# S5 state-space layer beside a Mish MLP: dense-1 weights of all seven groups prepared in one earlier block

## The chip, the cores and the metric

The kernel runs on one core of one Trainium2 chip. The metric is the device time of one launch in microseconds (us). A core has a matrix engine (PE, with its weight loads shown as PEld), a vector engine (VE; the profile calls it DVE), a scalar engine (ACT), a general engine (POOL) and a queue engine (SP) that only issues transfers. Each runs its own list of instructions in order and waits on semaphores; ACT, POOL and SP also issue DMAs from their places in that list, so a DMA waits for whatever stands ahead of it there.

## The reference

With x of 2048 rows and 1024 columns, and xn its layer norm over the columns, three terms are added:

```python
xn = _layernorm(x)
# state space: 1024 complex states, diagonal recurrence over the 2048 rows
Lam_bar = exp(dt * Lam)
B_bar = ((Lam_bar - 1.0) / Lam)[:, None] * Bmat
Bu = einsum("bld,pd->blp", xn, B_bar)
h[t] = Lam_bar * h[t - 1] + Bu[t]
y = 2.0 * einsum("blp,dp->bld", h, Cmat).real + xn * Dskip
# dense, 1024 -> 3584 -> 1024
a = einsum("bsd,df->bsf", xn, w1) + b1
act = a * tanh(softplus(a))                  # Mish
out = x + y + einsum("bsf,fd->bsd", act, w2)
```

Types are bf16 in and out.

## The kernel before, in words

**Blocks.** The rows are worked in four blocks of 512. The text counts them 1 to 4; in the code `blk` is 0 to 3. Each block has these stages on PE: dense 1 (x times w1, 28 tiles f of 128 columns), the input product (x times B, real and imaginary), dense 2 (Mish output times w2) and the output product (states times C, `proj`, three of whose eight slices j come last and finish the rows quarter by quarter). Between the input and the output product VE rotates the input (`rotate_in`), runs the recurrence as a scan (`recur`, eight slices j) and rotates back. Dense 2 and the output product add into the same eight banks of PSUM; `finish` adds them to x in `xx`, and the rows are stored.

**Quarter products.** A product of a 1024-deep operand can be made from four half-size pieces by Winograd's form of Strassen's scheme: seven products of half the width instead of eight. The input product is done so from block 2 on (`product`, `evacuate`, L871 to L939), dense 1 for some groups of four tiles (`w_product`, `w_evacuate`, L945 to L1019). The seven products of a group are numbered 1 to 7; letters in the order strings name the group: a to d are pairs of slices of the input product, p q s w x y z the seven groups of w1. The left operands are sums of parts of xnT, four arrays TT made by `sums_x`. The right ones (units) are prepared once: the group's 1024x512 of w1 is loaded in four quarters (`w_load`, POOL), its magnitude found (`w_abs`, ACT), carried across partitions through DRAM (`w_row_out`, `w_row_in`), turned into a power of two (`w_exponent`, VE), used to scale the quarters in place (`w_scale`, ACT), and three of the four scaled quarters are stored to DRAM (`wsd`, units 1, 2, 4); VE makes four sums in f16 (`w_sums`, units 5, 6, 3, 7), also stored. Later blocks read the units through the ring.

**Who prepares what, before.** Block 2 does dense 1 plainly (28 tiles) and prepares groups 3 to 6. Block 3 does groups 0 to 2 plainly (12 tiles, `NPL`), groups 3 to 6 by quarter products, and prepares groups 0 to 2 after its dense 2 has freed `act`. Block 4 does all seven by quarter products. Some sums of groups 0 and 1 are kept as closures and run as VE steps `k` in block 4; stores that aren't urgent are kept in `held` and `later`.

**The ring.** Weights come through `ring`, seven slots of 2048 columns. `items` lists all loads in order of use (w1, units `ws`, w2, and `c`, the rescaled C); `item_done` issues the load seven items ahead, on SP, into the slot just freed. SP also issues the transposes: x after its layer norm (`transpose_dma`), B (`transpose_B`), C (`transpose_C`). All of these share one order.

**Block 1.** Its first seven tiles are computed on raw x for the first 256 rows and corrected (`raw_scale`, `raw_add`, `hraw`). The tables of sines and cosines come from POOL phases (`phases`) and ACT (`table`). After phase 3, POOL issues the loads of x of block 2, whose statistics VE makes at tiles 14, 16, 18, 20 (`ln_stats_only`). During dense 2, VE runs the recurrence and scales C (`scale_C`), then B is scaled to a common range per state (`rows_scale`, `rows_spread`, `scale_B`), with two small DMAs on POOL for each half, and ACT writes the rescaled C to DRAM (`rows_C`).

**Layer norm of the next block.** In blocks 2 and 3 ACT makes the statistics (`next_stats`), the root (`next_root`, with two VE operations) and the scaled rows (`next_scale`); SP transposes them. `ln_skip` (VE) adds the skip term.

**The order inside a block** is written by hand in strings such as

```python
    WHOLE = HEAD + " d3 c7 d7 u7 c4 r2 u5 d4 u6 u4 r3 r4 r5 r6 r7"
```

where r is a rotation, u an early piece of dense 2, g a Mish over a range of tiles. `side(f)` hangs other work between the tiles of dense 1.

Of the kernel before, what the change touches and what calls it, by code (L numbers as in the profile page):

```python
# [5 lines left out]
ALU = mybir.AluOpType  # L6
# [3 lines left out]
P = 128  # L10
# [153 lines left out]
def build_kernel(nc, A_x, A_Lambda_re, A_Lambda_im, A_B_re, A_B_im, A_C_re, A_C_im,  # L164
# [21 lines left out]
    WHOLE = HEAD + " d3 c7 d7 u7 c4 r2 u5 d4 u6 u4 r3 r4 r5 r6 r7"  # L186
# [3 lines left out]
    PARTS = "a2 a1 b2 b1 a5 b5 a6 b6" + LATE  # L190
    FULL = ("p1 p5 k0 p2 k0 q1 q5 p6 q2 k0 s1 p7 k0 s5 p3 k0 q6 k0 s2 k0 p4 q7 k0 q3 h0 s6 q4 g0 a2 a1 s7 s3 b2 b1 s4 g1 a5 b5 a6 b6" + LATE)
    QUADS = "pqswxyz"
    NWQ = len(QUADS)
    NV = NPL // 4
    assert NV == 3
    W_BANKS = ((0, 2, 1), (3, 2, 4), (7, 2, 6), (3, 5, 7), (1, 5, 6), (4, 5, 7), (3, 5, 6))
    PLACE = {blk: (3, 4, 5, 6, 2, 0, 1) if blk == NB - 1 else (0, 1, 2, 3, 4, 5, 6) for blk in range(NB)}

    def w_items(order, place):
        units = [(place[QUADS.index(o[0])], int(o[1])) for o in order.split() if o[0] in QUADS]  # L200
        return [("ws", tuple(units[i:i + 2])) for i in range(0, len(units), 2)]

    W_ITEMS = {blk: w_items(FULL if blk == NB - 1 else PARTS, PLACE[blk]) for blk in SPLIT}

# [100 lines left out]
    wsm_v = late("wsm_v", [P, 4, NV], f32, 0)  # L305
    wsm_w = late("wsm_w", [P, 4, NWQ - NV], f32, 192)

    def wsm(n, lo, hi):
        return wsm_v[:, n, lo:hi] if lo < NV else wsm_w[:, n, lo - NV:hi - NV]

# [6 lines left out]
    ROWS = ((NV, NV + 2), (NV + 2, NWQ), (0, NV))  # L317
    wmd = [nc.dram_tensor("wmd%d" % h, [P, hi - lo], f32, kind="Internal").ap() for h, (lo, hi) in enumerate(ROWS)]
    b_wmd = [Buf("wmd%d" % i) for i in range(len(ROWS))]
    b_wmx = [Buf("wmx%d" % i) for i in range(len(ROWS))]  # L320
# [70 lines left out]
    for blk in range(NB):  # L391
        n1 = 0 if blk == NB - 1 else NPL if blk in SPLIT else NF
        items += [("w1", g) for g in range(n1 // 2)]
        items += W_ITEMS.get(blk, [])
        items += [("w2", 2 * PLACE[blk][g // 2] + g % 2) for g in range(NF // 2)]
        items += [("c", j) for j in range(NJ)] if blk >= FAST else []
# [280 lines left out]
    for b in [b for bs in b_wsm + b_ln + b_si_i + [b_sbf, [b_rv]] for b in bs]:  # L677
        b.readers = dict(b_st.readers)
# [55 lines left out]
    def turns():  # L734
# [3 lines left out]
        small("xc", "xs", "xc", ALU.max)  # L738
        aop(lambda e: e.activation(c("s1"), c("xs"), AF.Sin, scale=TWO_PI, bias=kon[:, 1:2]),
# [78 lines left out]
    def first_tile(blk, f):  # L818
        bank = f % 8
        if blk in SPLIT:  # L820
            bank = (0, 1, 2, 3, 5, 1, 4, 0, 6, 2, 3, 7)[f]
# [13 lines left out]
        if raw and f == 0:  # L835
            aop(lambda e: e.activation(act[:, 0:NR, 0:2 * P], hraw[:, 0:NR, :], AF.Mish),
                reads=b_hbf[0:4], writes=b_actf[0:NR])
# [3 lines left out]
    def places(blk, f, n):  # L841
        if blk in SPLIT:
            return (hb[:, f:f + n, :], b_hbf[f:f + n]) if f < NPL else (act[:, f - NPL:f - NPL + n, :],
                                                                        b_actf[f - NPL:f - NPL + n])
        return act[:, f:f + n, :], b_actf[f:f + n]
# [99 lines left out]
    def w_product(blk, i, n):  # L945
# [4 lines left out]
        s, half = n_item[0] % NRING, units.index((PLACE[blk][i], n))  # L950
# [20 lines left out]
    def w_evacuate(blk, i, n, keep):  # L971
        X, Y, Z = W_BANKS[i]
        at = PLACE[blk][i]
# [52 lines left out]
    W_RAW = (("a", 0), ("a", 8), ("h", 8), ("h", 0), ("h", 8), ("a", 0), ("a", 8))  # L1026
    W_SUM = (("a", 22), None, ("a", 16), ("a", 16), ("a", 22), ("a", 16), ("a", 22))
    held, later, steps = [], [], []

    def w_sum_at(i):  # L1030
        if i == 1:
            return [("a", 20), ("h", 12), ("h", 14), w_raw(i, 1, 0)]
        kind, t = W_SUM[i]
        return [(kind, t + 2 * n) for n in range(3)] + [w_raw(i, 1, 0)]
# [20 lines left out]
    def w_abs(i):  # L1055
        if i < NV:
            kind, t = w_raw(i, 0, 0)
            v, b_v = (hb, b_hbf) if kind == "h" else (act, b_actf)
            aop(lambda e: e.activation(CT[:, :, 1, TB:D], v[:, t:t + 8, :], AF.Abs, accum_out=wsm(0, i, i + 1)),  # L1059
                reads=b_v[t:t + 8], writes=b_snap + [b_wsm[0][i]])  # L1060
            return
        for ci in range(2):
            src, b_src = w_half(i, ci)
            aop(lambda e, src=src, ci=ci: e.activation(
                CT[:, 0:4, 1, TB:D], src.rearrange("p (j t) -> p j t", j=4), AF.Abs, accum_out=wsm(ci, i, i + 1)),
                reads=b_src, writes=b_snap[0:2] + [b_wsm[ci][i]])

    wmx_v = nc.alloc_sbuf_tensor_at("wmx_v", [P, NV * P], f32, offset=base_hb)

    def wmx(h):  # L1070
        n = ROWS[h][1] - ROWS[h][0]
        return (wmx_v[:, :] if n == NV else snaps[:, 4 + h % 2, D - TH:D - TH + n * P]), n

    def w_row_out(h):
        lo, hi = ROWS[h]
        a = wsm(0, lo, hi)
        if lo >= NV:
            b = wsm(1, lo, hi)
            vop(lambda e: e.tensor_tensor(a, a, b, op=ALU.add),
                reads=b_wsm[0][lo:hi] + b_wsm[1][lo:hi], writes=b_wsm[0][lo:hi])  # L1080
        PO.dma(lambda e: e.dma_start(wmd[h], a), DmaSem(nc, "d_wmd%d" % h),
               reads=b_wsm[0][lo:hi], writes=[b_wmd[h]])

    def w_row_in(h):
        dst, n = wmx(h)
        if n < NV:
            b_wmx[h].writer, b_wmx[h].readers = b_snap[2].writer, dict(b_snap[2].readers)
# [37 lines left out]
    def w_sums(i):  # L1125
# [3 lines left out]
        for n, o, b_o, x, b_x, y, b_y, op in ((5, s1, b_s1, il_, b_il_, ih_, b_ih_, ALU.add),  # L1129
# [3 lines left out]
            if n == 3:  # L1133
                y = y.bitcast(f16)
# [489 lines left out]
```

## Time and profile before

| what | us |
|---|---|
| median of 3 runs | 618.59 (616.88 to 618.75) |
| the profiled execution, its own time | 616.63 |
| its span, first to last instruction | 615.4 |
| PE busy | 598.0 |
| VE busy | 455.6 |
| ACT busy | 286.8 |
| POOL busy | 136.0 |

The stages on PE in that execution: dense 1 of block 1 until 61.1, input product until 88.8, dense 2 until 137.5, output product until 164.7; block 2 from there to 313.5, with its input product at 213.1 to 235.8; block 3 from 313.5 to 469.7, plain part of dense 1 until 334.2 and output product from 431.3; block 4 from 469.7 on, its dense 1 and input product until 534.6.

How to read it: the page's table of groups gives for each line, engine and operation the count, the busy time, the mean of one in ns, and the idle time of the engine just before, with what ended it. A timeline lists instructions in order of time (start, length, engine, line, operation; "<-" names what ended a wait, in us). A wait for several semaphores is put down to the one that came last by the profile; where that engine had long been done, it was another, often a DMA.

### The profile page before, as it was taken

Reading aid. Unit: us, or ns where it says so; the run is one execution under the profiler, and the core shown is the slowest. Engines: PE = TensorE matmul, PEld = TensorE weight load, DVE = VectorE, ACT = ScalarE, POOL = GpSimd, SP = SyncE. Lnnn points to the kernel's source line nnn. Section 1 sums busy time; section 2 is a strip of 40 time slices with the busy share of each in tenths; the row PEclk is TensorE's granted clock in tenths of the full one; section 3 lists DMA queues with packets and bytes.
Section 4 is the critical chain, followed back from the end, with each engine's and each line's share of the span. In section 5 each row is a group of like instructions: output and inputs, shape, how many; then the busy total and the mean of one; then the engine's idle time right before and its main releaser. Section 6 shows DMA issues by size and latency. Waiting matters only on the chain.

```text
span 615.4 us, 9103 instructions
## 1 busy us (share of the span) xinstructions
PE 598.0 (97%) x3467; PEld 341.6 (56%) x3511; DVE 455.6 (74%) x733; ACT 286.8 (47%) x371; POOL 136.0 (22%) x172
## 2 busy tenths in 40 slices
PE   8899999999999999999999999999959999999998
PEld 7544444444444586444445888444416888844444
DVE  6924797999999069997476776896099777689923
ACT  4639804379864315992723046305958714620000
POOL 2899100220128000211528000013012410000000
PEclk9999999999999999999999999999989999999999
DMA  9989999992697710889995457559287965864421
GB/s 247 299 201 180 209 216 247 283 310 84 194 310 257 234 49 4 293 182 258 353 333 197 175 156 263 198 174 295 78 226 271 402 244 152 260 204 138 164 76 69
DMA packets 109606, 130.59 MB, mean 212 GB/s; under 512 B 54154, under 2 KB 72202, under 8 KB 109562
## 3 DMA queue, kind: packets, MB, share of 16 engines
q1 hardware_dynamic: 97312, 93.41, 52.7%
q0 software_dynamic: 9136, 29.31, 14.6%
q10 hardware_dynamic: 3114, 7.29, 3.1%
q8 instruction: 28, 0.46, 0.3%
q14 instruction: 16, 0.13, 0.1%
HBM read 96.68 MB, written 21.24 MB: 192 GB/s over the span
## 4 chain that ended last, share of the span: by engine, by line
PE 88%; ACT 4%; DVE 3%; issue 2%; DMA 2%; SPq 1%; DVEq 0%; ACTq 0%
PE ps L1231 42%; PE ps L827 17%; PE ps L895 12%; PE ps L965 11%; PE ps L1177 4%; ACT CT L1059 1%; DMA ring<-in_B_w_dram 1%; PE ps L647 1%; DVE hT L1196 1%; DMA act<-in_B_w_dram 1%; ACT xn L550 1%; ACT hb L1120 1%; ACT act L1120 1%; PE ps L638 0%; DVE mt L1201 0%
## 5 line engine op out<-in xcount | busy, mean ns | idle before, releaser
L1231 PE MATMUL ps<-ring,act 128*128 128x512 bf16 x690 | 152.0, 379 | 0.7
L1231 PEld LDWEIGHTS ps<-ring,act 128*128 128x128 bf16 x704 | 68.9, 98 | 82.5
L827 PE MATMUL ps<-xnT,ring 128*128 128x512 bf16 x477 | 105.2, 379 | 3.6 <-issue 3.0
L1231 PE MATMUL ps<-ring,hT 128*128 128x512 bf16 x369 | 84.1, 386 | 7.7 <-DVE wsm_v L1103 6.7
L827 PEld LDWEIGHTS ps<-xnT,ring 128*128 128x128 bf16 x488 | 47.7, 98 | 60.6 <-issue 3.4
L1231 PEld LDWEIGHTS ps<-ring,hT 128*128 128x128 bf16 x378 | 37.3, 99 | 54.0 <-DVE wsm_v L1102 7.2
L1196 DVE TENSOR_TENSOR_SCAN hT<-cs,qi,hT 128x512 bf16<-128x512 f32 x48 | 58.9, 1269 | 0.0
L985 ACT ACTIVATE snaps<-ps,par,wsm_w 128x256 f32<-128x256 f32 x46 | 25.2, 562 | 52.4 <-PE ps L965 51.6
L838 ACT ACTIVATE act<-ps,par 128x512 bf16<-128x512 f32 (+1 forms) x56 | 34.5, 669 | 29.7 <-PE ps L827 29.5
L965 PE MATMUL ps<-TT,ring 128*128 128x256 f16 x352 | 44.0, 273 | 0.0
L1047 POOL DMA_DIRECT2D act<-in_B_w_dram x16 | 12.0, 748 | 144.5 <-PE ps L1231 96.1
L1231 PE MATMUL ps<-ring,hb 128*128 128x512 bf16 x186 | 42.2, 379 | 0.3
L1201 DVE TENSOR_TENSOR mt<-hT,tab 128x1024 bf16<-128x1024 bf16 x64 | 41.4, 688 | 1.1
L910 DVE COPY snaps<-ps 128x512 f32<-128x512 f32 x30 | 20.1, 686 | 24.5 <-PE ps L895 24.4
L965 PEld LDWEIGHTS ps<-TT,ring 128*128 128x128 f16 (+1 forms) x352 | 34.4, 98 | 5.0 <-issue 0.2
L965 PE MATMUL ps<-xnT,ring 128*128 128x256 bf16 x264 | 33.9, 273 | 0.8 <-DVE xx L1307 0.8
L861 DVE TENSOR_TENSOR mt<-hT,tab 128x1024 bf16<-128x1024 f16 x48 | 30.9, 686 | 0.4
L1231 PEld LDWEIGHTS ps<-ring,hb 128*128 128x128 bf16 x192 | 18.7, 98 | 21.1 <-DMA ring<-in_B_w_dram 0.4
L1307 DVE TENSOR_TENSOR xx<-ps,xx 128x1024 bf16<-128x1024 f32 (+1 forms) x16 | 18.5, 1187 | 16.0 <-PE ps L1231 16.0
L920 DVE TENSOR_TENSOR hT<-ps,snaps 128x512 f16<-128x512 f32 x36 | 24.6, 690 | 6.7 <-PE ps L895 4.3
L965 PEld LDWEIGHTS ps<-xnT,ring 128*128 128x128 bf16 (+1 forms) x264 | 25.8, 98 | 4.6 <-issue 1.3
L1231 PE MATMUL ps<-CT,hT 128*128 128x512 bf16 x126 | 27.7, 379 | 0.1
(212 smaller groups left out, 885.0 us busy)
## 6 DMA issues: line engine op xcount, KB each, us to landing
ring<-in_B_w_dram SPq DMA_DIRECT2D x90, 512.0 KB, 4.6
ring<-wsd SPq DMA_DIRECT2D x77, 256.0 KB, 4.5
ring<-ctd SPq DMA_DIRECT2D x24, 512.0 KB, 3.5
wsd<-act POOLq DMA_DIRECT2D x35, 256.0 KB, 6.4
ctd<-act ACTq DMA_DIRECT2D x8, 512.0 KB, 4.4
act<-in_B_w_dram POOLq DMA_DIRECT2D x16, 256.0 KB, 4.5
wsd<-hb POOLq DMA_DIRECT2D x14, 256.0 KB, 4.7
xx<-in_A_x_dram POOLq DMA_DIRECT2D x12, 256.0 KB, 7.6
```

The source lines that it names most:

```text
L827: PE.mm(lambda e, k=k, w=w: e.matmul(ps[:, bank, :], lhsT=w, rhs=xnT[:, k, :], start=k == 0, stop=k == NK - 1), reads=[b_ring[s]] + b_xnT, ...
L838: aop(lambda e: e.activation(at[0][:, ts], ps[:, bank, ts], AF.Mish, bias=b1(f)), reads=[b_ps[bank], b_par], writes=[at[1]])
L861: vop(lambda e, s=s: e.tensor_tensor(mt[:, s, :, :], hT16[:, :, j, :], tab[:, s, j, :].unsqueeze(1).to_broadcast([P, 2, TB]), op=ALU.mult) ...
L895: PE.mm(lambda e, w=w, x=x, o=o, begin=begin, end=end: e.matmul(ps[:, bank, o:o + TH], lhsT=w, rhs=x, start=opens and begin, stop=end, ski ...
L910: vop(lambda e: e.tensor_copy(dst, bank(b)), reads=[b_ps[b]], writes=[b_snap[i]])
L920: vop(lambda e: e.tensor_tensor(dst, bank(b), src, op=ALU.add), reads=[b_ps[b], b_src], writes=b_hT[ci][j0:j0 + 2])
L965: PE.mm(lambda e, w=w, x=x, o=o, begin=begin, end=end: e.matmul(ps[:, bank, o:o + TH], lhsT=w, rhs=x, start=opens and begin, stop=end, ski ...
L985: aop(lambda e, o=o, p=p, j=j: e.activation(o, p, AF.Identity, scale=ig, bias=b1(f0 + j)), reads=[b_ps[b], b_par, b_ig], writes=b_dst)
L1177: PE.mm(lambda e, j=j, ci=ci, k=k, bank=bank: e.matmul(ps[:, bank + ci, :], lhsT=BT[:, ci, j, k, :], rhs=xnT[:, k, :], start=k == 0, stop= ...
L1196: vop(lambda e, ci=ci, init=init: e.tensor_tensor_scan(out=hT[:, ci, j, :], data0=cj("r", j).to_broadcast([P, TB]), data1=hT[:, ci, j, :], ...
L1201: vop(lambda e, s=s: e.tensor_tensor(mt[:, s, :, :], hT[:, :, j, :], tab[:, s, j, :].unsqueeze(1).to_broadcast([P, 2, TB]), op=ALU.mult), ...
L1231: PE.mm(lambda e: e.matmul(ps[:, u, :], lhsT=lhsT, rhs=rhs, start=st_, stop=last), reads=reads, writes=[b_ps[u]], first=st_, last=last, te ...
```

## The change

The whole preparation moves ahead by up to one block:

- In block 1, VE takes the largest magnitude of groups 3 to 6 directly from the ring slots while plain dense 1 uses them (`w_most`, two reductions per group), and `w_row(0)` carries them across. The result is turned into exponents during dense 2. At the end of block 1, POOL loads groups 3 and 4 into `hb`, and ACT scales group 3.
- In block 2, groups 4, 5, 6 are scaled, summed and stored during dense 1, from `side(f)`; groups 0 to 2 are loaded, sized by ACT (`w_abs`), scaled and summed during dense 2 and the recurrence.
- Sums are made in place, over the scaled quarters, so each waits for the store of the unit it overwrites. `held`, `later` and `steps` are gone; output rows are stored by ACT in every block.
- Blocks 3 and 4 both run dense 1 entirely in quarter products, with one order (`SEVEN`).
- In block 1 the two sines of `turns` move behind tile 2, and the large Mish of `hraw` behind tile 7.
- The smaller scratch arrays move into the no longer used rows of `cs`; magnitudes are maxima rather than sums, with the exponent 12 instead of 13.

Cut to its core:

```diff
-    PARTS = "a2 a1 b2 b1 a5 b5 a6 b6" + LATE
-    FULL = ("p1 p5 k0 p2 k0 q1 q5 p6 q2 k0 s1 p7 k0 s5 p3 k0 q6 k0 s2 k0 p4 q7 k0 q3 h0 s6 q4 g0 a2 a1 s7 s3 b2 b1 s4 g1 a5 b5 a6 b6" + LATE)
+    HEAD1 = HEAD.replace("a2 a1 b2 b1", "k5 a2 a1 b2 b1 k6").replace("c6 c3", "n0 n1 c6 c3")
+    WHOLE = HEAD1 + " d3 c7 d7 u7 c4 r2 u5 d4 u6 u4 r3 r4 r5 r6 r7"
+    SEVEN = "p1 p5 p2 q1 q5 p6 q2 s1 p7 s5 p3 q6 s2 p4 q7 q3 s6 q4 g0 a2 a1 s7 s3 b2 b1 s4 g1 a5 b5 a6 b6" + LATE
+    REAL = (3, 4, 5, 6, 0, 1, 2)
...
+    def w_most(i, h):
+        s = (2 * i + h) % NRING
...
+        vop(lambda e: e.tensor_reduce(out=wsm(h, i, i + 1), in_=ring[:, s, :], axis=mybir.AxisListType.X, op=ALU.max,
+                                      apply_absolute_value=True), reads=[b_ring[s]], writes=[b_wsm[h][i]])
...
+    W_RAW = (("h", 0), ("h", 8), ("a", 0), ("h", 0), ("h", 8), ("h", 0), ("h", 8))
...
     def w_sums(i):
...
+        for n, o, b_o, x, b_x, y, b_y, op in ((5, ih_, b_ih_, il_, b_il_, ih_, b_ih_, ALU.add),
+                                              (7, il_, b_il_, rl_, b_rl_, il_, b_il_, ALU.subtract),
+                                              (6, rl_, b_rl_, ih_.bitcast(f16), b_ih_, rl_, b_rl_, ALU.subtract),
+                                              (3, rh_, b_rh_, rh_, b_rh_, rl_.bitcast(f16), b_rl_, ALU.subtract)):
+            vop(lambda e, o=o, x=x, y=y, op=op: e.tensor_tensor(o.bitcast(f16), x, y, op=op),
+                reads=b_x + b_y, writes=b_o)
+            w_store(i, n, o, b_o)
...
         def side(f):
             if blk:
-                at = (1, 3, 5, 7) if blk in SPLIT else (8, 10, 12, 15)
+                at = (8, 10, 12, 15)
...
                 if blk == FAST:
...
+                    if f == 4:
+                        w_scale(4)
+                    if f in (7, 11):
+                        w_sums(3 + (f - 7) // 4)
+                    if f == 16:
+                        w_load(5)
+                        w_load(6)
+                    if f in (21, 24):
+                        w_scale(5 + (f - 21) // 3)
                 return
+            if f == 2:
+                turn_sines()
+            if f == NR:
+                aop(lambda e: e.activation(act[:, 0:NR, 0:2 * P], hraw[:, 0:NR, :], AF.Mish),
+                    reads=b_hbf[0:4], writes=b_actf[0:NR])
...
+            if f >= 4 * ROWS[0][0] and f % 4 < 2:
+                w_most(f // 4, f % 4)
+            if f == 26:
+                w_row(0)
...
-        for f in range(0 if blk == NB - 1 else NPL if blk in SPLIT else NF):
+        for f in range(0 if blk in SPLIT else NF):
...
         if near and blk not in SPLIT:
             for q in range(NQ):
                 next_stats(blk + 1, q)
+            w_abs(0)
+            w_abs(1)
...
                 if near and j == 1:
...
-                    for i in (0, 2, 1):
-                        w_load(i)
-                    w_abs(0)
                     for q in range(NQ):
                         next_stats(blk + 1, q)
-                    w_abs(2)
-                    w_abs(1)
-                    w_row_out(2)
-                    w_row_in(2)
...
                 if j == 1:
                     next(out_stage)
...
+                    w_load(2)
+                    w_abs(2)
+                    w_row(1)
+                if j == 6:
+                    w_exponent(1)
+                    for i in (0, 1, 2):
+                        w_scale(i)
                 continue
             if j == 0:
                 ln_root()
+                w_exponent(0)
...
+        if near:
             for q in range(NQ):
                 ln_skip(blk + 1, q)
...
             for n in range(4):
                 sums_x(n, VE)
...
         if blk == FAST:
...
+            for i in (0, 1, 2):
+                w_sums(i)
...
             for j in range(NJ):
                 rows_C(j)
+            for i in (3, 4):
+                w_load(i)
+            w_scale(3)
         for _ in out_stage:
             pass
```

In the order strings, `k5` and `k6` now call `w_sums(5)` and `w_sums(6)`, `n0` and `n1` call `w_load(0)` and `w_load(1)`. On POOL the loads and stores of this preparation stand in the order of these calls, between the loads of x (`load_x`) and, in block 2, the four `sums_x`.

## The prediction

> Blocks are counted 1 to 4. Times are us in the profiled execution before, on its own clock unless "after" is said. "VE" is the page's DVE.
>
> **What bounds the kernel now.** PE is busy 598.0 of 615.4 us, so I first looked for the places where PE isn't at full pace. The groups of PE by line show two: "3.0 idle" in dense 1 of block 1 and "6.7 idle" in the output product of block 3 (matmuls of L1231 on hT). The timeline of PE and the table of windows place them:
>
> ```profile
> 26.45 4.91 PE L827 MATMUL ps<-xnT,ring 128*128 128x512 bf16 x22 [2.98 <-issue]
> ...
> 431.32 18.29 PE L1231 MATMUL ps<-ring,hT 128*128 128x512 bf16 x82
> 450.15 1.04 PE L1231 MATMUL ps<-ring,hT 128*128 128x512 bf16 x4 [0.53 <-DVE hT L1204]
> 457.92 10.96 PE L1231 MATMUL ps<-ring,hT 128*128 128x512 bf16 x39 [6.73 <-DVE wsm_v L1103]
> 469.66 1.03 PE L965 MATMUL ps<-xnT,ring 128*128 128x256 bf16 x8 [0.79 <-DVE xx L1307]
> ```
>
> ```profile
> 61.14:88.77 27.63, 27.52 (x128) 12.53 (x128) 21.82 (x28) 13.32 (x20) 2.70 (x2) 1.00 1.12 215
> ...
> 313.51:334.24 20.73, 20.62 (x97) 9.45 (x97) 17.37 (x17) 8.73 (x12) 12.93 (x10) 1.00 0.72 252
> ...
> 431.32:469.66 38.34, 30.14 (x126) 12.78 (x128) 23.03 (x45) 30.06 (x28) 5.64 (x10) 0.91 0.54 160
> 469.66:534.57 64.91, 64.90 (x592) 57.95 (x594) 48.33 (x74) 35.20 (x52) 9.59 (x18) 1.00 0.78 272
> ```
>
> Columns: start, length, PE, PEld, VE, ACT, POOL, clock, DMA. 128 matmuls of 512 columns take 27.63 unhindered and 38.34 in block 3: 10.71 lost, 8.05 as idle time (0.53+6.73+0.79), the remaining 2.66 at the lower clock (0.91 over this window). The chain of waits says why:
>
> ```profile
> 418.19 4.41 DMA act<-in_B_w_dram
> 422.64 3.50 issue
> 426.14 0.19 ACT CT L1059
> ...
> 440.20 3.71 ACT CT L1059 x2
> 443.93 1.28 ACT L558
> ```
>
> and the timeline of SP what follows:
>
> ```profile
> 447.23 6.58 SPq L578 DMA_TRANSPOSE xnT<-xn  x4
> 453.90 0.53 SPq L422 DMA_DIRECT2D ring<-ctd  x1
> ```
>
> w1 of groups 0 to 2 is loaded as dense 2 frees `act`; ACT sizes it ahead of the layer norm (until 443.7); VE waits 19.9 for its root; the transposes of xn wait; behind them on SP waits the last load of C. That load, issued at 453.90, lands 3.9 later, 457.8, which is where PE resumes. The "VE L1103" of the row had merely ended then.
>
> **The change, part by part.**
>
> (a) Block 3 no longer prepares groups 0 to 2. The 29.5 that ACT waits for their load go, `next_stats` starts with the end of Mish (about 393), root and scale follow recurrence 5 (425.6) at once, the SP queue reaches the transposes at 432 instead of 447, and the last C load at about 438.5, ten before its first use (431.3 + 17.3). VE: recurrences end at about 435, skip and sums of x (4x1.3 + 4x0.7) at 443.5, before PE's first finished banks (451). Gain 10.71.
>
> (b) Dense 1 of block 3: 96 matmuls in 20.73 become 168 quarter matmuls at 64.91/600 = 0.1082: 18.18. Gain 2.55. Block 4 computes the same products as before; its VE sums (`k`) lay under PE.
>
> (c) Block 1, sines. The 2.98 stall: tile 8 needs bank 0, whose Mish stood on ACT behind the sines (21.9), a table load and the large Mish of `hraw`. Now Mish of tiles 0 to 2 precedes the sines: PE runs on and ends dense 1 at 58.2 instead of 61.1.
>
> (d) Block 1, sizing. Eight reductions of 128x2048 on VE, a form that the trace doesn't show. Lower bound 1.22 (two-input bf16 of 2048, L1406); upper 3.31 (reduction of 256 in 0.414, L1098, times 8). L1307 on PSUM takes 0.691 for 512 and 1.220 for 1024, 1.03 ns an element; carried on, 2048 is 2.28. I take 2.3, the one with an element's pace. They don't only cost 18: between the second and third stand `ln_stats` 0 and 1, which wait for x of block 2 (landed 51.3 to 58.2). Ring slots 1 to 6 are reloaded only after their reduction, in SP's order, with the transposes of B and C behind them. Since PE is 3 ahead and items 15 and 16 aren't queued yet, I let x land 3 earlier (bound: unchanged, or 4). Then VE: 53.1, two reductions 57.7, statistics 61.0, four reductions 70.2; the drains of the input product start at 70.3 instead of 64.6, 3.1 each. PE waits 0.7 for the first of its four bank pairs, and 1.3 and 1.0 at dense 2. So the 3 gained are given back: PE at 94 is where it was (bounds with reductions of 1.2 and 3.3: 3 early, 6 late). VE, with 2.0 more for `w_exponent(0)`, reaches the scaling of C, which idled 4.2 for its DMA, about 1 late. Call this lateness v = 1 (bounds -3 and +7). C keeps 4 before its use by PE.
>
> (e) Block 2, ACT. The weightiest edit. `w_scale(3)` now stands on ACT between the copies of C and the first Mish:
>
> ```profile
> 171.76 0.37 ACTq L1399 DMA_DIRECT2D ctd<-act  x1
> 172.45 2.83 ACTq L1293 DMA_DIRECT2D out_dram<-xx  x4
> 175.37 1.28 ACT L838 ACT_TABLE_LOAD   x1 [3.63 <-DVE BT L1406]
> 176.66 6.07 ACT L838 ACTIVATE act<-ps,par 128x512 bf16<-128x512 f32 x10
> ```
>
> and it waits for `w_load(3)`, which on POOL stands behind both DMAs of `rows_scale(1)`:
>
> ```profile
> scd<-sbf POOLq DMA_DIRECT2D x1, 1.0 KB, 5.6
> ...
> hb<-in_B_w_dram POOLq DMA_DIRECT2D x8, 256.0 KB, 5.2
> ...
> wsd<-act POOLq DMA_DIRECT2D x9, 256.0 KB, 7.0
> ```
>
> POOL issued the second at 166.0. After: 167.0, then four loads at 0.75, the last issued at 169.8, landing 175.3 (5 to 5.5). Two scalings at 1.92: 179.4. Output stores 2.8, table load 1.3: first Mish done at 184.1. PE wants its bank for tile 8 at 164.74 + 8x1.727 = 178.5: a stall of 5.6.
>
> Does the clock fall with it? The trace has 2.98 without a fall and 6.73 with one that cost 2.66. 5.6 is nearer the second: PE is 8.2 late (bounds 5.6 and 8.2). [...] Going by either, the sum moves by 0.1, because the next wait lies as far.
>
> (f) The next wait: `w_scale(5)` and `w_scale(6)` stand behind Mish 21 and 24. `w_load(5)` waits its turn on POOL: after the three stores of group 3 come the x loads (each waits for an output store, 6.6 to landing: until 188.8), stores of group 4 (until 190.9), stores of the sums of group 3 (193.1), two TT (198.1), the sums of group 4, on VE, which wait for the store of their own input (landing 195.5) and run beside a TT (200.9), two more TT, each with its `ln_skip` as before in 3.2 (207.3). So loads of group 5 are issued 207.3 to 210.3, landing 214.5. ACT: 3.9 (218.4), Mish 22 to 24 (220.2), 3.8 (224.0), Mish 25 at 224.7. Product b2 needs that bank, at 216.6 before: 8.1 late. (e) and (f) overlap, PE is late by the greater: 8.2.
>
> (g) Rest of block 2, all 8.2 later. In ACT's order `w_abs(0)`, `w_abs(1)` and two table loads precede the root: 249 + 10.2 + 1.3 + 7.6 + 1.6 = 269.7, while VE stands there at 267: 2.7 lost on VE, covered. VE then: recurrences, `w_exponent(1)`, skip, sums of x, carry, twelve sums of groups 0 to 2 at 0.69: free at 316. The first finished banks must be added by 321.8 - 1.2. Margin 4.6; if it is gone, each us of VE costs one. Two late VE sums (5.4) vanish. At block 3's start the first products have their weights (group 3) and TT.
>
> Sum: 616.63 - 10.71 - 2.55 + 8.2 = 611.6 on the profiled execution. The three runs' median, 618.59, lies 2.0 above that execution; 618.59 with the same gain of 5.1 is 613.5. I predict between them, **612.6**. About 0.3%, 1.9 us, can be told from no change.
>
> **The rivals.**
>
> Forecast: 2 to 9 faster, chance 0.53.
>
> A, loads land as early as their issue allows (v = -3, POOL chain 4 shorter, lateness 4): 616.6 - 13.3 + 4 = 607.4. For it: DMA is at 0.13 to 0.35 share in parts of 190 to 235. Against: 0.95 to 1.06 at 175 to 190. Chance 0.08.
>
> B, reductions at the upper price: v = 7, PE 6 later everywhere in block 2, lateness 12 to 14: 616.6 - 13.3 + 13 = 616.4, no change. For it: 0.649 for 384 in the reduction of block 3, worse than proportional. Against: that one reads with a stride. Chance 0.14.
>
> C, slower: POOL's queue is longer than (f) says. Six steps there wait for a landing or VE. The median of wsd stores in the busy stretch is 7.0, not 5; with 2 more on each of four landings in series and 1 on the two pairs of TT, group 5 lands at 224, Mish 25 ends at 234.5, lateness 18: 616.6 - 13.3 + 18 = 621.3. It decides from a landing later than 223, 1.9 over the balance. For it: nothing hides an ACT that waits in order in front of Mish. Against: after 190 the DMAs have air. Chance 0.20.
>
> D, the boundary of block 3 isn't freed (another late thing, such as x of block 4 or ring loads of wsd, holds PE by 5): 616.6 - 13.3 + 5 + 8.2 = 616.5. For it: every ring load stands in one SP queue. Against: x is loaded 60 before use. Chance 0.05.
>
> **Numbers.** Faster: forecast, A, and a tenth of B and D, 0.62. Same: most of B and D, 0.15. Slower: C and the tail of B, 0.23. The range takes in A at 607.4 and most of C: 606.5 to 620.5, less than 2 in 10 left out. The forecast alone: 608 to 615.
>
> **What would show it.** Right: no idle time at tile 8 of block 1; 38.34 down to about 27.7; a stall of 5 to 6 in dense 1 of block 2 with its clock below 1, released by ACT; SCALE rows of groups 5 and 6 holding Mish 22 and 25; reductions at 2.3. Wrong: PE waiting at the start of block 3 for VE's sums, a stall in front of C in block 1, or a wait of VE for a wsd store that PE feels.

## The result, and the profile after

The changed kernel takes 620.75 us in the median of 20 runs, the kernel before 618.49 in 20 runs beside them. The ratio is 1.0041, 95% interval 1.0023 to 1.0058: slower by 0.4%, where 1% faster was forecast. Its runs lie further apart (616.7 to 623.2; one more, at 627.4 with a mean granted clock of 0.984 against 0.989 to 0.994 in the others, counts as slow and is left out of the ratio) than those of the kernel before (616.1 to 619.2). Its profiled execution took 617.87, with a span of 616.3.

The windows of the stages show gain and loss (columns: start and end, length, busy time of PE, PEld, VE, ACT, POOL, clock, DMA, GB/s). First dense 1 and the input product of block 2 in the kernel before:

```profile
164.58:212.93 48.35, 48.09 (x221) 21.92 (x225) 34.53 (x34) 24.96 (x31) 18.64 (x17) 1.00 0.82 264
212.93:239.97 27.04, 26.99 (x237) 23.09 (x236) 19.86 (x34) 4.78 (x8) 0.00 (x0) 1.00 0.11 40
```

Then the same two stages in the changed kernel, and the output product of block 3:

```profile
163.61:217.99 54.38, 50.19 (x224) 22.18 (x225) 41.05 (x43) 34.39 (x34) 32.83 (x41) 0.97 1.00 344
217.99:252.53 34.54, 30.28 (x238) 24.29 (x236) 24.72 (x42) 11.12 (x15) 12.42 (x20) 0.90 0.60 206
...
442.56:470.18 27.62, 27.62 (x129) 12.54 (x128) 15.65 (x27) 0.00 (x0) 0.00 (x0) 1.00 0.59 173
```

Against the same stages before: the output product of block 3 falls from 38.34 to 27.62, all that it could. Block 3 as a whole falls from 156.3 to 144.3. Block 1 is 1.0 shorter. But in block 2 dense 1 takes 54.38 instead of 48.35 and the input product 34.54 instead of 27.04, both at a clock below 1: 13.5 lost. With 0.4 in block 4 the span is 0.9 longer.

The timeline of PE shows where (start, length, what ended the wait before it):

```profile
163.61 13.97 PE L816 MATMUL ps<-xnT,ring 128*128 128x512 bf16 x64 [0.23 <-DVE xx L1251]
181.77 36.38 PE L816 MATMUL ps<-xnT,ring 128*128 128x512 bf16 x160 [4.19 <-ACT act L824]
217.99 1.91 PE L880 MATMUL ps<-xnT,BT 128*128 128x256 bf16 x16
224.00 3.57 PE L880 MATMUL ps<-xnT,BT 128*128 128x256 bf16 x16 [4.11 <-ACT act L824]
227.37 4.94 PE L880 MATMUL ps<-TT,SS 128*128 128x256 f16 x32
232.46 1.92 PE L880 MATMUL ps<-xnT,SS 128*128 128x256 bf16 x16 [0.15 <-DVE snaps L895]
...
252.53 3.83 PE L1182 MATMUL ps<-ring,act 128*128 128x512 bf16 x17
```

Two waits for a Mish, and the 16 products behind the second take 3.57 where 16 otherwise take 1.91: the granted clock, which the trace records beside the instructions, is at half from 182.19 to 185.61 and from 223.15 to 229.98. The timeline of ACT shows what the two Mish stand behind:

```profile
175.73 2.00 ACT L1085 ACTIVATE hb<-hb,cs 128x2048 bf16<-128x2048 bf16 x1 [3.49 <-DMA hb<-in_B_w_dram]
...
179.65 1.28 ACT L824 ACT_TABLE_LOAD   x1
180.94 3.00 ACT L824 ACTIVATE act<-ps,par 128x512 bf16<-128x512 f32 x5
...
213.88 3.90 ACT L1085 ACTIVATE hb<-hb,cs 128x2048 bf16<-128x2048 bf16 x2 [5.37 <-DMA hb<-in_B_w_dram]
217.69 1.82 ACT L824 ACTIVATE act<-ps,par 128x512 bf16<-128x512 f32 x3
219.39 3.89 ACT L1085 ACTIVATE hb<-hb,cs 128x2048 bf16<-128x2048 bf16 x2
223.18 1.84 ACT L824 ACTIVATE act<-ps,par 128x512 bf16<-128x512 f32 x3
```

L1085 is `w_scale`. At 175.73 ACT had waited 3.49 for the load of group 3, at 213.88 it had waited 5.37 for that of group 5; Mish 25, the one that product b2 needs, is the first of the last row and ends at 223.9.

### The profile page after: what moved, and what is told of

Read it like the earlier page. It is cut to its first block, busy times and chain, and to the rows that moved or that the text cites. A ratio compares the mean times of both kernels' runs of the same rounds, so it can differ in the third digit from the quotient of the medians.

```text
span 616.3 us, 9311 instructions
## 1 busy us (share of the span) xinstructions
PE 601.0 (98%) x3583; PEld 349.3 (57%) x3583; DVE 476.8 (77%) x748; ACT 278.6 (45%) x367; POOL 122.6 (20%) x162
## 4 chain that ended last, share of the span: by engine, by line
PE 59%; DVE 16%; DMA 9%; SPq 6%; POOL 5%; issue 3%; ACT 2%; ACTq 0%; POOLq 0%; DVEq 0%
PE ps L1182 37%; PE ps L950 12%; PE ps L880 11%; SPq L799 4%; DVE hT L1147 3%; DMA xx<-in_A_x_dram 2%; DVE CT L787 2%; DMA wsd<-hb 2%; DVE CT L784 2%; DMA out_dram<-xx 2%; ACT snaps L970 2%; DVE hb L1097 2%; DVE mt L1152 1%; DVE cs L1044 1%; POOL py L709 1%
## 5 line engine op out<-in xcount | busy, mean ns | idle before, releaser
L816 PE MATMUL ps<-xnT,ring 128*128 128x512 bf16 x392 | 86.8, 384 | 4.4 <-ACT act L824 4.2
L970 ACT ACTIVATE snaps<-ps,par,cs 128x256 f32<-128x256 f32 x80 | 43.3, 562 | 99.6 <-PE ps L950 49.9
L816 PEld LDWEIGHTS ps<-xnT,ring 128*128 128x128 bf16 x392 | 38.6, 99 | 52.2 <-issue 7.6
L950 PE MATMUL ps<-TT,ring 128*128 128x256 f16 x448 | 55.8, 273 | 0.4 <-ACT snaps L970 0.4
L950 PEld LDWEIGHTS ps<-TT,ring 128*128 128x128 f16 (+1 forms) x448 | 43.7, 98 | 6.8 <-issue 0.9
L950 PE MATMUL ps<-xnT,ring 128*128 128x256 bf16 x336 | 42.9, 273 | 0.0
L1085 ACT ACTIVATE hb<-hb,cs 128x2048 bf16<-128x2048 bf16 x12 | 23.3, 1998 | 24.5 <-DVE cs L1074 15.6
L987 DVE SCALAR_TENSOR_TENSOR act<-ps,cs,snaps 128x512 bf16<-128x512 f32 x24 | 18.0, 751 | 17.2 <-PE ps L950 15.7
L1097 DVE TENSOR_TENSOR hb<-hb 128x1024 f16<-128x1024 bf16 (+1 forms) x24 | 17.6, 735 | 17.6 <-DMA wsd<-hb 17.0
L1079 POOL DMA_DIRECT2D wsd<-hb x42 | 22.7, 543 | 40.1 <-ACT hb L1085 30.7
```

The lines of the kernel that those rows point to most:

```text
L816: PE.mm(lambda e, k=k, w=w: e.matmul(ps[:, bank, :], lhsT=w, rhs=xnT[:, k, :], start=k == 0, stop=k == NK - 1), reads=[b_ring[s]] + b_xnT, ...
L950: PE.mm(lambda e, w=w, x=x, o=o, begin=begin, end=end: e.matmul(ps[:, bank, o:o + TH], lhsT=w, rhs=x, start=opens and begin, stop=end, ski ...
L970: aop(lambda e, o=o, p=p, j=j: e.activation(o, p, AF.Identity, scale=ig, bias=b1(f0 + j)), reads=[b_ps[b], b_par, b_ig], writes=b_dst)
L1085: aop(lambda e, t=t: e.activation(t, t, AF.Copy, scale=wsm(2, i, i + 1)), reads=b_t + [b_wsm[2][i]], writes=b_t)
L1097: vop(lambda e, o=o, x=x, y=y, op=op: e.tensor_tensor(o.bitcast(f16), x, y, op=op), reads=b_x + b_y, writes=b_o)
```

## The experiments

All times are medians; the interval is that of the ratio to the kernel before, in runs beside it. "C lands" is the last landing of C's transposes in block 1, "5 lands" the last landing of the load of group 5, "dense 2" the start of dense 2 of block 2 on PE, all in the profiled execution.

| run | what | us | ratio (95%) | C lands | 5 lands | dense 2 |
|---|---|---|---|---|---|---|
| after | the change | 620.75 | 1.0041 (1.0023 to 1.0058) | 101.6 | 213.86 | 252.53 |
| e1 | scaling of 3 later | 626.64 | 1.0147 (1.0117 to 1.0176) | 101.6 | 221.62 | 260.29 |
| e2 | scalings of 5, 6 later | 620.69 | 1.0058 (1.0031 to 1.0084) | 101.7 | 213.75 | 253.02 |
| e3 | both | 617.14 | 0.9975 (0.9952 to 0.9999) | 100.6 | 223.82 | 249.93 |
| e4 | PE filled at b2 | 623.26 | 1.0105 (1.0070 to 1.0139) | 103.0 | 217.75 | 258.83 |
| f1 | loads of 3, 4 first | 624.53 | 1.0104 (1.0079 to 1.0129) | 99.3 | 217.73 | 256.40 |
| f2 | e3, x loads later | 614.67 | 0.9955 (0.9930 to 0.9980) | 106.2 | 220.81 | 252.12 |
| f3 | f2, 5 and 6 in turn | 612.92 | 0.9915 (0.9890 to 0.9940) | 103.3 | 209.30 | 246.34 |
| f4 | before, C's load first | 621.14 | 1.0040 (1.0024 to 1.0055) | 97.0 | | |
| g1 | statistics later | 615.06 | 0.9965 (0.9949 to 0.9981) | 96.2 | 207.92 | 249.00 |
| g2 | before, sines alone | 613.63 | 0.9940 (0.9924 to 0.9956) | 91.8 | | |
| g3 | f3, sums moved | 607.56 | 0.9835 (0.9807 to 0.9862) | 102.5 | 209.17 | 241.40 |
| g4 | g3 and g1 | 602.86 | 0.9762 (0.9745 to 0.9778) | 96.3 | 202.63 | 236.39 |
| h1, h2 | the change again | 621.06, 620.99 | one run each | 101.1, 102.4 | 216.07, 216.51 | 255.26, 255.36 |
| h3 | e1, x loads later | 624.45 | 1.0105 (1.0077 to 1.0134) | 99.5 | 212.61 | 254.18 |

**e1, e2, e3: the two scalings, one at a time.** e1 takes `w_scale(3)` from the end of block 1 into `side`:

```diff
-            w_scale(3)
...
-                    if f == 4:
-                        w_scale(4)
+                    if f in (3, 5):
+                        w_scale(3 + (f - 3) // 2)
```

> Changed kernel with w_scale(3) taken from between the copies of C and the first Mish of block 2 to behind Mish 3, and w_scale(4) from behind Mish 4 to behind Mish 5. Theory (two gates one behind the other, the second sets the lateness): the stall of 4.2 at tile 8 goes with its 1.7 at half clock, but the loads of group 5 on POOL hang on the x loads and on VE's sums and land near 214 as before, so b2 meets the same Mish 25 near 223 to 224 after a longer idle time, 9 to 10 instead of 4.1: dense 2 of block 2 starts at 251 to 253 as before, and the time stays within 2.5 of the changed kernel's. Rival (the first gate is the whole cost and the second only its echo): the stall at b2 does not grow, and the time falls by 6 to 12.

The first wait is gone (dense 1 of 48.5), and the kernel is 6 slower. Neither the theory nor the rival had that. PE now idles 17.79 at b2:

```profile
231.76 3.57 PE L880 MATMUL ps<-xnT,BT 128*128 128x256 bf16 x16 [17.79 <-DVE snaps L895]
```

The timeline of POOL tells why; first the changed kernel's, then e1's:

```profile
178.03 1.11 POOL L1079 DMA_DIRECT2D wsd<-hb  x2 [6.67 <-ACT hb L1085]
...
206.12 5.97 POOL L1024 DMA_DIRECT2D hb<-in_B_w_dram  x8
```

```profile
183.24 0.55 POOL L368 DMA_DIRECT2D xx<-in_A_x_dram  x1 [12.15 <-DMA out_dram<-xx]
...
186.73 3.21 POOL L1079 DMA_DIRECT2D wsd<-hb  x6
...
214.44 5.96 POOL L1024 DMA_DIRECT2D hb<-in_B_w_dram  x8
```

With the scaling called later, its stores stand on POOL behind the loads of x of block 3, which wait for the output stores to land. VE's sums of group 3 follow 9 later (195.77 instead of 186.63), and the loads of groups 5 and 6 are issued 8.3 later. The table holds a plain rule for the kernels that keep the changed kernel's order behind that load: dense 2 starts 38.67 behind the landing of group 5 in the changed kernel, in e1 and in f1, to the hundredth, whether tile 8 waited or not. It is the least of the distances seen: in g1, which keeps the order too, PE waits 2.21 more for VE's copies and the distance is 41.08.

e2 takes the two others behind the last Mish:

```diff
-                    if f in (21, 24):
-                        w_scale(5 + (f - 21) // 3)
+                    if f == 27:
+                        w_scale(5)
+                        w_scale(6)
...
-    HEAD1 = HEAD.replace("a2 a1 b2 b1", "k5 a2 a1 b2 b1 k6").replace("c6 c3", "n0 n1 c6 c3")
+    HEAD1 = HEAD.replace("c1 r0 d5 d1 r1 c6 c3", "c1 k5 r0 d5 d1 r1 k6 c6 n0 n1 c3")
```

> Changed kernel with w_scale(5) and w_scale(6) behind Mish 27, and the sums and loads that follow (k5, k6, n0, n1) some 14 to 19 products later in the input product. Theory: the idle 4.1 at b2 and the clock's fall behind it (3.0 to 3.4) go, dense 2 of block 2 starts at 245 to 246 instead of 252.5, and the time falls by 7 to 7.5. Rival (VE, busy from 242 to 321 with hardly a gap, takes the wait over): VE waits for the stores of groups 5 and 6 at the later places, the end of block 2 waits for VE's first addition, and less than 4 is won.

The wait at b2 is gone, but no time is won. The timeline of PE in e2:

```profile
241.25 1.05 PE L880 MATMUL ps<-TT,BT 128*128 128x256 f16 x8 [1.36 <-ACT snaps L897]
...
247.12 1.89 PE L880 MATMUL ps<-TT,BT 128*128 128x256 f16 x8 [3.54 <-DVE hT L905]
```

The rival was right in the main: VE does its sums of groups 5 and 6 (5.7) at a place where it has no idle time, PE waits 1.36 and 3.54 for VE's additions (the first by way of a copy on ACT, which itself waits 3.59 for VE), and the clock falls for 6.83 there.

> Both moves together. Theory: no idle time over 1 in block 2 and no fall of the clock, dense 1 of 48.4, input product of 27 to 28, dense 2 of block 2 at 240 to 241; 11.5 to 12.5 less than the changed kernel, 604 to 605 in a profiled execution and 11 under the kernel before. Its runs also spread less, by under 3 instead of 6.5, if it is the length of the two waits that varies from run to run. Rival (the gates only hide a third wait, VE's sums of groups 5 and 6 behind the stores, or the sums of groups 0 to 2 ahead of the first additions): 4 to 8 less, with idle time at the end of block 2 or at the start of block 3.

3.6 less than the changed kernel, a little under the rival's 4 to 8 and far from the theory, and the spread did not shrink (612.2 to 621.2). PE waits 1.81 and 3.53 near the end of the input product, as the rival had it. The stores of group 3 again stand behind the loads of x.

**e4: does the clock fall because PE idles?** A step `f38` in the order string makes 38 products of 128x256 into a free bank, which nobody reads:

```diff
-    HEAD1 = HEAD.replace("a2 a1 b2 b1", "k5 a2 a1 b2 b1 k6").replace("c6 c3", "n0 n1 c6 c3")
+    HEAD1 = HEAD.replace("a2 a1 b2 b1", "k5 a2 a1 f38 b2 b1 k6").replace("c6 c3", "n0 n1 c6 c3")
```

> Changed kernel with 38 products of 128x256 that nobody reads put on PE between a1 and b2 of block 2 (38 x 0.108 = 4.1, the length of the idle time there). Theory (the clock falls because PE idles over 3 at b2): b2 starts near 224 as before, give or take 0.5, but the clock stays at 1.0 behind it, and the time falls by 3 (2.5 to 3.5). Rival (the second fall has another cause, the first one's echo say): the clock falls at about 223 all the same, and the time stays or grows by up to 1.

b2 starts 10.14 behind the landing of group 5, as in the changed kernel, and the clock stays at 1 there: PE's idle time was the cause. But nothing is won: the median is 2.5 above the changed kernel's, against the theory. PE at full pace reaches VE's sums of group 6 too soon, waits 3.06 for VE, and the clock falls for 3.41 there. This execution's first wait was also longer (6.47).

**f1, h3: the head of the chain.** f1 puts `w_load(3)` and `w_load(4)` ahead of `rows_scale(1)` on POOL.

> Changed kernel with one edit: on POOL w_load(3) and w_load(4) stand ahead of the two transfers of rows_scale(1) instead of behind them; w_scale(3) stays where it is on ACT. Theory (one chain, load - scaling - stores - sums - load - scaling - stores - sums, runs through POOL, ACT and VE, and PE's lateness is that of the chain): w_load(3) is issued from 158.3 (VE's last use of hb) instead of 165.4, w_scale(3) waits for nothing, tile 8 waits 0.5 to 1.5 instead of 4.2 with no fall of the clock, and everything behind, Mish 25 too, comes 3 to 3.5 earlier: dense 2 of block 2 at 249, the time 3 to 4 less. Rival (scd(1), issued 3.7 later, holds VE's scaling of B and so the sums of group 3): Mish 25 comes no earlier, idle time at b2 grows by what tile 8 saves, and the time is within 1 of the changed kernel's.

Tile 8 waits 0.25, under the theory's 0.5 to 1.5, but the time is 3.8 above the changed kernel's, more than the rival's 1. The rival's mechanism held: the store of `scd`, 1 KB, issued behind the eight loads, landed 12.0 after its issue (4.0 in the changed kernel), VE waited 10.2 for it and came to the sums of group 3 at 189.95 instead of 186.63.

h3 is e1 with the x loads taken from the end of `tail` to behind `w_load(6)`:

```diff
-        if blk + 2 < NB and blk != FAST:
-            for q in range(NQ):
-                load_x(PO, blk + 2, q)
...
                     if f == 16:
                         w_load(5)
                         w_load(6)
+                        for q in range(NQ):
+                            load_x(PO, blk + 1, q)
```

> e1 with the four loads of x of block 3 behind w_load(6) on POOL. Theory: e1 lost because the stores of group 3 stood behind these loads; without them w_load(5) is issued at 205 to 208 and not at 214.4, and the time falls by 5 to 9 from e1's 626.64, back to the changed kernel's or a little under it. Rival (VE's or ACT's order makes e1 slow): w_load(5) is still issued later than 211 and the time stays over 623.

The issue came at 204.94, as expected, so POOL's order was what delayed e1's loads. The time fell by only 2.2 in the median (6.1 between the two profiled executions). PE, early at b2, idles 10.71, and half clock takes 10.24 and later 3.41. Why four of its other five runs are 4 to 7 slower than the profiled one stays open.

**f2, f3, g3: the chain mended.** f2 is e3 with the same edit of the x loads.

> e3 (both scalings moved) and the four loads of x of block 3 moved on POOL from the end of block 1 to behind w_load(6). Theory: in e1 and e3 the stores of group 3 stood behind these loads, which wait for the output stores to land (issued at 187 instead of 181); with the loads away the chain is 6 to 8 earlier than in e3: w_load(5) issued at 205 to 207 instead of 213.6, no wait of VE for groups 5 and 6, dense 2 of block 2 at 241 to 243 instead of 249.9, and the time 7 to 9 less than e3's. Rival (it is VE's own work ahead of the input product, 11 of sums and skips until 218.5, and not the stores): VE's first copy of the product still comes at 217 to 219, dense 2 at 247 or later, less than 3 won.

2.5 won in the median, less than the theory's 7 to 9. PE's two waits of e2 (1.35 and 3.54) are there again, as the rival said. The execution profiled, 618.35, is one of f2's slower ones: its C landed at 106.2, which cost PE 4.21 at the end of block 1.

f3:

```diff
+                    if f == 11:
+                        w_load(5)
                     if f in (7, 11):
                         w_sums(3 + (f - 7) // 4)
                     if f == 16:
-                        w_load(5)
                         w_load(6)
-                    if f == 27:
-                        w_scale(5)
-                        w_scale(6)
+                    if f in (23, 27):
+                        w_scale(5 + (f - 23) // 4)
```

> f2 with w_load(5) ahead of w_sums(4) on POOL (behind Mish 11), w_scale(5) behind Mish 23, w_scale(6) behind Mish 27. Theory of the chain: groups 5 and 6 now come one after the other, w_load(5) is issued at 195 to 199, w_scale(5) at 205 without a wait, and VE's sums of group 5 find their stores landed; dense 2 of block 2 at 240 to 242, 0 to 2 less than f2. Rival: POOL, blocked by w_load(5) until the stores of the sums of group 3 have landed, brings the sums of x and of group 4 later, and the time is 1 to 3 more than f2's.

1.8 less than f2, as expected; group 5 lands at 209.30. But dense 2 starts at 246.34 and not at 240 to 242: the two waits for VE remain (1.36 and 3.54), this time without a fall of the clock. g3 moves the sums, and the loads of x of block 3 to behind `w_scale(6)`:

```diff
-    HEAD1 = HEAD.replace("c1 r0 d5 d1 r1 c6 c3", "c1 k5 r0 d5 d1 r1 k6 c6 n0 n1 c3")
-    WHOLE = HEAD1 + " d3 c7 d7 u7 c4 r2 u5 d4 u6 u4 r3 r4 r5 r6 r7"
+    HEAD1 = HEAD.replace("a7 b7", "a7 b7 k5").replace("c6 c3", "n0 c6 c3")
+    WHOLE = HEAD1 + " d3 c7 d7 u7 c4 r2 u5 d4 u6 u4 k6 n1 r3 r4 r5 r6 r7"
```

> f3 with VE's sums of group 5 behind b7 and those of group 6 behind u4 of the input product (in f3 behind c1 and r1), the loads of x of block 3 behind w_scale(6), w_load(0) ahead of c6 and w_load(1) behind the sums of group 6. Theory: in f3 PE waits 1.36 and 3.54 in the input product because VE, which has no idle time from 230.6 on, does 5.7 of sums there; with the sums where VE idles (225.4) and behind the last product, the input product takes 27 to 28.5 instead of 32.3 and the time is 3 to 5 less than f3's: 608 to 610. Rival (VE has no idle time left anywhere in block 2, only the place of the wait moves): as much is lost at the end of block 2, before VE's first addition to the output, and less than 1.5 is won.

5.4 won, and the input product takes 28.3: the theory, with a little more than its 3 to 5. One wait of 1.07 for VE is left there.

**g1: block 1.** The statistics of x of block 2 go behind the last reduction:

```diff
-            if f in (14, 16, 18, 20):
-                ln_stats_only(1, (f - 14) // 2)
...
+            if 27 <= f < 31:
+                ln_stats_only(1, f - 27)
```

> Changed kernel with one edit in block 1: the four statistics of x of block 2 (ln_stats_only) stand on VE behind the eight reductions and not among them. Theory: in the changed kernel VE waits 8.9 for that x with six reductions behind it, the ring loads behind these reductions stop SP from 44.5 to 53.3, and the transposes of C stand behind them; C's last landing sets the start of block 2 (landing + 62.0 wherever it is later than 100.6). With the edit SP does not stop, C lands at 95 to 99 instead of 101.6 (up to 106.2 in other executions), block 2 starts at 161 to 162.5 in every execution, and the median falls by 2 to 4 under the changed kernel's 620.75. Rival (C's landing is set by the traffic of the DMAs and not by the SP queue): it still lands at 100.5 or later, and the median moves by less than 1.

5.7 less than the changed kernel, more than the theory's 2 to 4, and 0.35% faster than the kernel before. The timelines of VE and of SP in the changed kernel, then that of VE in g1:

```profile
34.56 4.47 DVE L1044 TENSOR_REDUCE cs<-ring 128x1 f32<-128x2048 bf16 x2
47.91 1.42 DVE L517 BATCH_NORM_STATS2 stats<-xx 128x6 f32<-128x512 bf16 x2 [8.88 <-DMA xx<-in_A_x_dram]
...
58.46 8.81 DVE L1044 TENSOR_REDUCE cs<-ring 128x1 f32<-128x2048 bf16 x4
```

```profile
41.27 3.23 SPq L793 DMA_TRANSPOSE BT<-in_A_B_im_dram  x1
53.33 2.55 SPq L411 DMA_DIRECT2D ring<-in_B_w_dram  x2
```

```profile
34.42 17.63 DVE L1044 TENSOR_REDUCE cs<-ring 128x1 f32<-128x2048 bf16 x8
...
52.16 1.41 DVE L517 BATCH_NORM_STATS2 stats<-xx 128x6 f32<-128x512 bf16 x2
```

VE waits 8.88 for x with reductions behind it, and SP, which may reload a ring slot only when it is sized, stops from 44.5 to 53.3 with every transpose of C behind it. In g1 the eight reductions run through and C lands 5.4 earlier.

**g2: the sines alone, in the kernel before.** The edit is the change's own.

> Kernel before with the edit of the sines alone (step c): both sines behind the Mish of tile 2, the Mish of hraw behind that of tile 5. Theory: the 2.98 of idle time at tile 8 of block 1 goes, but VE's scaling of C, tied to C's landing near 101, allows block 2 to start at 163 and no earlier, so 1 to 2 of the 3 are won, 616.5 to 617.5 in the median; the fall of the clock behind the 2.98, which comes in some executions only, goes too. Rival (PE alone sets block 1): all 3 are won, 615.5 or less.

The rival: 4.5 less in the median, 3.0 between the profiled executions. The fall of the clock fits the difference: f4, whose block 1 is that of the kernel before, has 3.41 of half clock behind tile 8 and starts block 2 at 166.44, 1.86 later than the profiled execution before; g2 has neither that wait nor that fall. My bound failed because C did not stay near 101; it landed at 91.8. (Why so early isn't shown: in f4 it landed at 97.0 with the order of before.) So the whole 3.5 at the start of block 2 (164.58 to 161.11) was to be had; the changed kernel starts it 2.5 later than g2, and g1 takes back 2.0 of that by moving the statistics alone.

**f4: the boundary of block 3, in the kernel before.** `tail` yields once the last load of C is queued, ahead of the transposes:

```diff
             if blk >= FAST:
                 item_done()
+            if blk == NB - 2 and j == 0:
+                yield
...
                 if near and j == 5:
+                    next(out_stage)
                     for q in range(NQ):
                         transpose_dma(q)
```

> Kernel before with one edit in block 3: the last ring load of C is put on SP ahead of the four transposes of xn instead of behind them. Theory of step (a) (PE waits at 450 to 458 for that load, not for VE L1103): the 6.73 of idle time in the output product of block 3 and the 2.66 at the lower clock go; VE, free at 457.9, is then what the first products of block 4 wait for, 1 to 3; the time falls by 6 to 9, to 609 to 612. Rival (the row's own releaser, VE's sums, holds PE): the idle time stays where it is or moves whole to the start of block 4, and less than 2 is won.

Nothing won, 0.4% lost. The wait for the load is gone, and others stand in its place in f4's timeline of PE:

```profile
452.33 1.04 PE L1231 MATMUL ps<-ring,hT 128*128 128x512 bf16 x4 [0.81 <-DVE hT L1204]
456.82 10.49 PE L1231 MATMUL ps<-ring,hT 128*128 128x512 bf16 x40 [3.46 <-DVE hT L1204]
471.84 1.87 PE L965 MATMUL ps<-xnT,ring 128*128 128x256 bf16 x8 [4.53 <-DVE xx L1309]
```

0.81, 3.46 and 4.53 for VE, 8.8 together, with the clock at half for 3.41 and 6.83. The load of C was the last link of a chain whose others, ACT's sizing, the root, VE's recurrence, are late as well: VE waits 20.20 for the root in f4, as it waits 19.90 before.

**h1, h2: why the median lies above the profiled execution.**

> The changed kernel once more, for another execution's trace. Theory: whatever its time, block 2 starts on PE 62 behind C's last landing (if that is later than 100.6), dense 2 of block 2 starts 38.7 to 41.1 behind the last landing of group 5, and the span is that start plus 363.8, within 1; the executions differ by these two landings alone. Rival: the span differs by more than 1 from that sum, so something else (another fall of the clock, a wait in blocks 3 and 4) varies.

> One more execution of the changed kernel, with the same theory as h1 (block 2 at C's landing + 62, dense 2 of block 2 at group 5's landing + 38.7 to 41.1, span 363.8 behind that) and the same rival.

Both took 621, the median. Block 2 starts at 163.06 and 164.38, 62.0 behind C's landing in both. Dense 2 of block 2 starts 39.2 and 38.9 behind the landing of group 5, and the span ends 364.3 and 364.1 behind that. The theory held: of the 3.2 by which these executions are longer, 2.2 and 2.7 are the later landing of group 5. The execution profiled first was one of the early ones. What makes that landing vary from execution to execution isn't shown.

**g4: both edits.**

> g3 and g1's edit together. Theory: both gains add: 605 to 607 in the median, 11 to 13 under the kernel before, no fall of the clock, and the runs within 3 of each other. Rival (block 1 is bound by VE, not by C's landing): nothing over g3.

602.86, 2.4% under the kernel before, its four runs within 0.8: both gains add, with 2 to 4 more than the theory had, and the rival (nothing over g3) is out. The windows of dense 1 and of the input product of block 2 in g4:

```profile
161.00:209.35 48.35, 48.35 (x226) 21.94 (x225) 41.15 (x42) 34.42 (x37) 28.70 (x35) 1.00 0.99 343
209.35:236.39 27.04, 27.04 (x237) 23.04 (x236) 22.35 (x38) 8.68 (x10) 10.49 (x18) 1.00 0.70 242
```

48.35 and 27.04, the lengths of the kernel before, with VE and POOL doing the work of the change beside them.

## Why the prediction was wrong

**What was right.** (a): 10.71 predicted, 10.72 measured. f4 adds that moving the last load of C alone doesn't win it. (c): the 2.98 went. (d): a reduction takes 2.2, predicted 2.3. (e): the first Mish ends at 181.6 and not at 184.1, the stall is 4.19, predicted 5.6, with a fall of the clock. (f): group 5 lands at 213.86, predicted 214.5; Mish 25 ends at 223.9, predicted 224.7, and PE resumes with it at 224.00.

**The step that failed is the lateness, 8.2,** from "Product b2 needs that bank, at 216.6 before: 8.1 late" and "(e) and (f) overlap, PE is late by the greater". That only the later gate counts is right: e1 and f1 lose the first wait and start dense 2 at the same distance behind the landing of group 5. But 12.56 was measured at dense 2, 4.4 more, from two terms:

- b2's due time. It follows 16 quarter products behind 212.93, at 214.67; my 216.6 was 1.9 late. As PE resumes 0.7 before my 224.7, 1.2 of it is left.
- The second wait and the clock behind it, priced at nothing. With PE 8.2 late from the first wait and b2 due at 216.6, the text saw no wait there. PE came out of dense 1 only 5.1 late, so it idled 4.1 at b2, and from 224.00 to 229.98 the products take 0.213 and not 0.109: 3.0 lost.

The remaining 0.2 is the wait for VE's copies.

**(b) was too large.** From the start of block 3 to its output product 1.32 was won (117.97 to 116.65), 2.55 predicted. 0.72 of the rest is two new waits (0.21 for ACT's copies, 0.51 for VE). Some 0.2 is the sum's own: its window of 64.91 shows 594 weight loads and not 600, so a product takes 0.109, and 168 take 18.4. In g4 the same stretch takes 118.17, with 1.7 of waits, most of them for ring loads. The last 0.3 stays open.

**(d) had the right price and the wrong place.** I named the ring slots and SP's order, and then counted the reductions as VE's time alone. Their cost is that SP waits for them, ahead of C: g1 wins 5.7 without taking one away. C's scaling was 0.5 later in the profiled execution, my v was 1; but C's landing runs from 99.3 to 106.2 over the executions with this block 1, and block 2 starts 62.0 to 62.3 behind it wherever it comes at 100.6 or later. My upper bound of 7 for v had this, the value taken did not.

**The sum.** 611.6 was worked out for the profiled execution and 617.87 measured: 4.4 of the 6.3 from the lateness, 1.2 from (b), 0.4 from block 4, 0.3 around the span. The step from the profiled execution to the median then added 2.9, where I had put 1.0. Rival C came nearest in time (621.3), but by a later landing, beyond 223; the landing was as forecast in that execution, and in the median ones some 2 to 3 later.

(e) judged the clock by the length of the wait. In these runs that length did not decide it: the same wait of 3.53 to 3.54 cost no half clock in f3, 3.41 of it in e3 and f2, and 6.83 in e2.

## What to carry to other kernels

Work that hides on paper beside a busy engine must be followed through every in-order queue as one chain, load to scaling to store to sum to the next load: here dense 2 of block 2 started 38.67 or a little more behind the landing of one load, and reordering the changed kernel took 17.9 off it with not one operation less. A gate taken away in front of a later gate wins nothing and lengthens the idle time there, so price each wait from its own due time, and the fall of the clock behind it as a range (none to 6.83 of half clock came behind the same 3.54 here). Ask of every new reader of a shared ring what it keeps the refilling queue from doing, and profile more than one execution before trusting the first.

## What the runs showed of the hardware

- Half clock came behind waits of PE, and no length of the wait decided it: 2.98 brought none in the kernel before and 2.97 brought 3.41 in f4, at the same tile 8 of block 1; 3.54 brought none in f3, and 2.21, at 227.27 in g1, brought 3.41. What decided it isn't shown. The falls lasted 3.41 and 6.83 in the changed kernel, one 6.83 in the kernel before (455.51 to 462.34) and one 10.24 in h3.
- One fall of the changed kernel began before PE resumed (223.15 against 224.00), the other after it (182.19 against 181.77). The one at 223.15 ran until 229.98 and so reached work that had waited for nothing: the 32 products that start at 227.37 took 4.94, 2.61 of it at half clock, where the same 32 take 3.66 in g4.
- A store of 1 KB landed 4.0 after its issue in the changed kernel, 5.6 in the kernel before and 12.0 behind eight loads of 256 KB in f1.
